# GpSimd takes columns of VectorE's second squaring, and a score burst may wait for VectorE's pair: one core of a gated attention and gMLP kernel

## The chip, the cores and the metric

The kernel runs on one core of a Trainium2 chip. The metric is the device time of one execution in microseconds (us). A core has five engines with a queue of instructions each: TensorE (PE in the profile; its weight loads are PEld), VectorE (DVE), ScalarE (ACT), GpSimd (POOL) and SyncE (SP). Each works through its own queue in order, and engines wait for each other by semaphores. A wait at the head of a queue holds up all that stands behind it.

## The reference

Two branches over the same input are mixed by a gate. The first is attention with 32 query heads of 16 columns over one shared key and value; the second is a gMLP with a mixing matrix over the sequence.

```python
S, D, H, Dh, F, Fh = 2048, 512, 32, 16, 1376, 688      # batch 1
g = sigmoid((x * gate_w).sum(-1, keepdims=True))

q = (x @ wq) as [32 heads, S, 16];  k = x @ wk;  v = x @ wv      # k, v: [S, 16]
p = softmax(q @ k.T * 16 ** -0.5)                                # [32, S, S]
a = (p @ v as [S, 512]) @ wo

z  = gelu(x @ w_in)
z2 = layernorm(z[..., Fh:])
b  = (z[..., :Fh] * (w_sp @ z2 + b_sp[:, None])) @ w_out

out = g * a + (1 - g) * b
```

## The kernel before

**Units and blocks.** Attention's scores are 32 x 2048 x 2048 numbers, and each of them needs an exponential. The work is cut into 32 units. A unit has 64 blocks: 16 tiles of 128 keys times 4 row groups g of TensorE, with 512 columns each. A score pair is two such blocks, two matmuls into two neighbouring banks of PSUM (`s_mm`, tag S).

**Two ways to an exponential.** ScalarE's way (`exp_op`, L579): one instruction reads a pair of banks (128 x 1024, fp32) and writes two slots of the tile P in bf16. It uses banks 0 to 3, two pairs in turn, so the pair for exponential k can be written once exponential k - 2 is done. VectorE's way goes through banks 4 and 5 (BD) and the tile X, which has NX = 5 buffers of 2048 columns in fp16. A batch is four blocks, which are two pairs. For each pair, `d_A` (L603, tag dA) writes a linear function of the scores into half a buffer; then two squarings of the whole buffer (L611, made by `d_poly`) follow. The first (dU) stays in fp16, the second (dW) writes bf16 in place. The square of a square of a linear function, with a small correction by two matmuls for each group (MC, CC), stands for the exponential. A unit gives at most NMAX = 7 of its 16 key tiles to VectorE.

**Values.** TensorE multiplies each block of P or X with V (`pv_mm`, `pv_raw`, tag PV) into bank 6, four row groups side by side, in waves. When a unit is complete, `norm` follows: VectorE transposes the bank into T1 (L623), GpSimd computes the reciprocal (rc, L629), multiplies it with the gate factor (rcg, L632) and scales (Tn, L635). For each second unit VectorE transposes Tn into OT (L638).

**The rest.** The second branch and the projections run as groups of matmuls through bank 7, with an evacuation on VectorE. The GELUs run in one stretch on ScalarE, between about 178 and 205 us, so that its table is loaded only once.

**What sets the order.** A planner in the kernel's own Python fixes the order of every queue before anything runs. It keeps a clock for TensorE, ScalarE and VectorE with assumed costs in ns, asks `pe_pick`, `act_pick` and `dve_pick` in turn for candidates, and takes the ready one with the lowest priority number. GpSimd's instructions go into its queue when the VectorE step that they belong to is chosen. Semaphore waits are derived from reads and writes of keys (`Prog.op`). An operation that needs an earlier one of its own engine waits on that engine's semaphore too, except on TensorE.

Details that matter here:

- `pe_pick` issues a score burst for ScalarE as soon as the banks are free. If VectorE's banks are free too (`d_ok`), VectorE's pair joins the burst behind ScalarE's two matmuls. A pair for VectorE alone is issued when there is time. `dl` is the latest time for the next burst: the planned end of the running exponential less SLATE = 451 ns. Other work for TensorE is only taken when it ends by then.
- `dve_pick` takes, in order of priority, evacuations, norms, dA, other small steps, and last the squarings. The queue of squarings, `polyq`, is strictly first in, first out, and a squaring is assumed to cost 78 + 0.5208 ns for each column.
- When dW ends, the batch's four blocks go to the list `avail` and may be taken into a wave of V matmuls. A batch m cannot begin before batch m - NX has given up its buffer.

Of the kernel before, what the change touches and what calls it, by code (L numbers as in the profile page):

```python
# [15 lines left out]
S = 2048  # L16
# [6 lines left out]
NU = 32  # L23
# [21 lines left out]
PJOIN = 1  # L45
APRI = 1.5
DMARG = 150.0
EMARG = 50.0
EXPT = (0, 478, 904, 1330)
SLATE = 451.0  # L50
# [112 lines left out]
def build_kernel(nc, x_d, wq_d, wk_d, wv_d, wo_d, win_d, wsp_d, bsp_d, wout_d, gw_d, out_d):  # L163
    es = ExitStack()
    with es:
# [423 lines left out]
        def pv_mm(blk, src, key):  # L589
            u, kt, g = blk  # L590
            pv_raw(u, g, V1[:, kt, :], src, [("V", kt // 4), key], "PV")

        def cor_mm(u, g, z):
            n = (64 - units[u]["hi"]) // 4
# [6 lines left out]

        def d_A(m, h):
            op("dve", lambda v: v.tensor_scalar(X[:, m % NX, 1024 * h:1024 * h + 1024], bank(BD, 1024), PA, PB, ALU.mult, ALU.add),  # L603
               r=[bkey(BD), bkey(BD + 1)], w=[("X", m % NX, h)], tag="dA")

        def d_poly(m, hs):

            w = 1024 * len(hs)
            x = X[:, m % NX, 1024 * hs[0]:1024 * hs[0] + w]
            ks = [("X", m % NX, h) for h in hs]  # L610
            return [(78 + 0.5208 * w, lambda d_=d_, tag=tag: op("dve", lambda v: v.tensor_tensor(d_, x, x, ALU.mult), r=ks, w=ks, tag=tag))  # L611
                    for d_, tag in ((x, "dU"), (x.bitcast(B16), "dW"))]

        def norm(pgx, u):
            o = pgx.op
            c, jp, jj = u // 8, (u % 8) // 2, u % 2
            pr = (u // 2) % 2
            t1 = T1[:, :].rearrange("p (b w) -> p b w", w=32)
            lsum = t1[:, :, 16:17]
            tn = Tn[:, pr, :].rearrange("p (b w) -> p b w", w=32)[:, :, 16 * jj:16 * jj + 16]  # L620

            def f_t1():
                o("dve", lambda v: v.transpose(T1[:], bank(BO)), r=[("bk", BO)], w=["T1"], tag="T1")  # L623

            def f_rc(e):
                if e == "dve":
                    o("dve", lambda v: v.reciprocal(rc[:].unsqueeze(2), lsum), r=["T1"], w=["rc"], tag="rc")
                else:
                    o("pool", lambda g: g.tensor_tensor(rc[:].unsqueeze(2), lsum, mone[:].unsqueeze(2), ALU.pow), r=["T1", "mone"], w=["rc"], tag="rc")  # L629

            def f_rcg(e):
                o(e, lambda v: v.tensor_tensor(rcg[:], rc[:], RHO[:, c, :], ALU.mult), r=["rc", ("RHO", c)], w=["rcg"], tag="rcg")  # L632

            def f_tn(e, s_, k):
                o(e, lambda v: v.tensor_tensor(tn, t1[:, :, 0:16], s_[:].unsqueeze(2).broadcast_to([128, 16, 16]), ALU.mult), r=["T1", k], w=[("Tn", pr, jj)], tag="Tn")  # L635

            def f_t2():
                o("dve", lambda v: v.transpose(OT[:, c, jp, :], Tn[:, pr, :]), r=[("Tn", pr, 0), ("Tn", pr, 1)], w=[("OT", c, jp)], tag="T2")  # L638

            if pgx is not pg:  # L640
                return [f_t1, lambda: f_rc("dve"), lambda: f_tn("dve", rc, "rc")] + ([f_t2] if jj else [])
            res = []
            if u < NU - 1:
                def f_all():
                    f_t1()
                    f_rc("pool")
                    f_rcg("pool")
# [69 lines left out]
        dpair = {"free": 0.0}  # L717
        da_q = deque()
        batches = []
        cur = {"m": None, "hs": []}  # L720
# [17 lines left out]
        def new_batch(now):  # L738
# [20 lines left out]
                return True  # L759
            return False  # L760

        def d_pair(now, used):

            if not cur["hs"] and not new_batch(now):
                return None
            m = cur["m"]
            u, kt = batches[m]
            fr = [h for h in cur["hs"] if 2 * h not in used]
            if not fr:
                return None  # L770
            h = fr[0]

            def take():
                cur["hs"].remove(h)
                for i in range(2):
                    s_mm(BD + i, (u, kt, 2 * h + i))
                dpair["free"] = None
                return (m, h)
            return take

        def d_ok(now):
            return dpair["free"] is not None and dpair["free"] + LAT + DMARG <= now and sum(x[0] for x in polyq) <= DPQ

        class Done(dict):
            def get(self, k):
# [11 lines left out]
        def pe_pick(now):  # L797
# [23 lines left out]
            elif ua < NU and edone.get(k - 2) is not None:  # L821
# [19 lines left out]
                if bl:  # L841
                    new = []

                    def emit():
                        T["now"] = now
                        tk = d_pair(now, [b[2] for b in bl]) if d_ok(now) else None
                        for i_, blk in enumerate(bl):
                            s_mm(EB[k % 2] + i_, blk)
                            units[blk[0]]["lo"] += 1
                        if tk:  # L850
                            new.append(tk())
                        stepb[k] = bl
# [197 lines left out]
        def act_pick(now):  # L1050
# [24 lines left out]
            if k in sdone:  # L1075
# [4 lines left out]
                if None not in fr:  # L1080
# [9 lines left out]
                    def f2(t_end):  # L1090
                        edone[k] = t_end
                        for i_, blk in enumerate(bl):
                            avail.append((blk, P[:, 512 * (pp + i_):512 * (pp + i_) + 512], ("P", pp + i_), t_end + LAT + PMARG, k, pp + i_))
                    cands.append((t, 1, EXPT[len(bl)], e2, f2))
            return cands

        def dve_pick(now):
            cands = []
            for q, pr in ((evac_q, 0), (norm_q, 1), (dve_q, 2)):
                if q:  # L1100
# [5 lines left out]

                    def e(q=q, f_=f_):
                        q.popleft()
                        f_()

                    def f(t_end, d_=d_):
# [3 lines left out]
            if da_q:  # L1115
                t, m, h = da_q[0]

                def e1():
                    da_q.popleft()
                    d_A(m, h)  # L1120

                def f1(t_end):
                    dpair["free"] = t_end
                    hs_ = [h]
                    if PJOIN:
                        if m not in half:
                            half[m] = h
                            return
                        hs_ = [0, 1]
                    u, kt = batches[m]  # L1130
                    for z, (c_, f_) in enumerate(d_poly(m, hs_)):
                        polyq.append((c_, f_, m, [(u, kt, 2 * h_ + i) for h_ in hs_ for i in range(2)] if z else []))
                cands.append((t, APRI, 1134, e1, f1))
            if polyq:
                cp_, fp_, mp, rel = polyq[0]

                def e2():
                    polyq.popleft()
                    fp_()

                def f2(t_end):
                    for blk in rel:
                        g = blk[2]
                        avail.append((blk, X[:, mp % NX, 512 * g:512 * g + 512].bitcast(B16), ("X", mp % NX, g // 2), t_end + LAT + PMARG, None, mp))
                cands.append((now, 4, cp_, e2, f2))
            return cands

        half = {}
# [3 lines left out]
        tend = {}  # L1152
        events = [T[k] for k in T if T[k] > 0]
        heapq.heapify(events)
        while True:
# [216 lines left out]
```

## Time and profile before

| | us |
|---|---|
| median of 14 runs | 758.3 |
| lowest and highest run | 755.06 and 767.85 |
| profiled execution | 758.58 |
| its span in the profile | 756.4 |

| engine | busy, us | share of the span |
|---|---|---|
| ScalarE | 734.7 | 97% |
| VectorE | 717.1 | 95% |
| TensorE | 688.2 | 91% |
| GpSimd | 137.3 | 18% |

The lines of the profile are read so. A group of instructions has its source line, engine, operation, the tiles that it writes and reads (output<-input), the shapes, and a count. Behind the first bar are the busy time in us and the mean length of one record in ns; behind the second, the time that the engine was idle just ahead of the group and what ended it. Records of neighbours on ScalarE and VectorE can overlap by some hundred ns: the distance from one start to the next is then shorter than a record. In a timeline, a line has the start in us, the length in us, the engine, and the instruction with its count. In a view by stretches, a line has the stretch, its length, the busy time with the number of instructions, TensorE's granted clock, and the share and rate of DMA.

Where the span ends: the last exponential starts at 745.83 us, and the last unit's norm, the last output projections and the stores take the rest. The GELU stretch holds ScalarE's exponentials from 178.81 to 205.22 us.

### The profile page before, as it was taken

How to read it: one execution, taken by the hardware profiler on the slowest of the kernel's cores; microseconds unless marked ns; L12 is line 12 of the kernel's file. 1: busy time of each engine (PE TensorE's matmuls, PEld its weight loads, DVE VectorE, ACT ScalarE, POOL GpSimd, SP SyncE). 2: the span in 40 equal slices, each digit the busy share in tenths (PEclk: the TensorE clock that was granted, in tenths of full speed). 3: DMA queues.
4: the chain of work that ended last, by engine and by line, in shares of the span. 5: the costliest groups of instructions: out<-in, count | busy, mean ns of one | idle time of the engine just before them, and what ended most of it. 6: DMA issues, size and time to landing. Idle time of an engine off the chain costs nothing.

```text
span 756.4 us, 13353 instructions
## 1 busy us (share of the span) xinstructions
PE 688.2 (91%) x5313; PEld 186.4 (25%) x5407; DVE 717.1 (95%) x784; ACT 734.7 (97%) x801; POOL 137.3 (18%) x112
## 2 busy tenths in 40 slices
PE   7889898889889999999999999899999999999996
PEld 2222222223322222222222222222222222222221
DVE  4599999999999999999999999999999999999996
ACT  5999999999899999999999999999999999999995
POOL 3111101212111111210221111012212112012120
PEclk9899999999999999999999999999999999999999
DMA  9810000000000000310000014000000600000000
GB/s 221 165 23 1 1 1 1 1 1 1 1 1 1 1 1 1 84 42 16 2 1 1 1 31 96 15 1 1 1 1 2 115 19 8 1 1 1 1 1 32
DMA packets 49045, 16.96 MB, mean 22 GB/s; under 512 B 44129, under 2 KB 48913, under 8 KB 48978
## 3 DMA queue, kind: packets, MB, share of 16 engines
q1 hardware_dynamic: 46066, 15.10, 9.2%
q10 hardware_dynamic: 2784, 0.69, 0.5%
q8 instruction: 44, 0.72, 0.4%
q0 software_dynamic: 128, 0.26, 0.2%
q14 instruction: 23, 0.19, 0.1%
HBM read 3.20 MB, written 2.10 MB: 7 GB/s over the span
## 4 chain that ended last, share of the span: by engine, by line
ACT 62%; issue 17%; PE 12%; DVE 7%; DMA 1%; POOL 1%; ACTq 0%
ACT P L579 59%; PE ps L298 8%; PE ps L297 4%; DVE X L603 3%; DVE X L611 2%; ACT z L492 1%; DMA wvg<-in_gate_w_dram 1%; ACT z L496 1%; POOL rc L629 0%; DVE T L623 0%; DVE outsb L556 0%; DVE MC L450 0%; DVE OT L638 0%; ACTq L151 0%; ACT L579 0%
## 5 line engine op out<-in xcount | busy, mean ns | idle before, releaser
L579 ACT ACTIVATE P<-ps 128x1024 bf16<-128x1024 f32 x770 | 707.6, 1152 | 4.0 <-PE ps L298 3.9
L298 PE MATMUL ps<-QA,KA 32*128 32x512 bf16 x2048 | 318.7, 385 | 49.1 <-ACT P L579 40.5
L603 DVE TENSOR_SCALAR X<-ps 128x1024 f16<-128x1024 f32 x254 | 308.8, 1216 | 7.8 <-PE ps L298 6.5
L611 DVE TENSOR_TENSOR X<-X 128x2048 f16<-128x2048 f16 x254 | 311.2, 1226 | 2.6
L629 POOL TENSOR_TENSOR rc<-T,mone 128x16 f32<-128x16 f32 x31 | 97.2, 3134 | 551.6 <-DVE T L623 551.6
L298 PEld LDWEIGHTS ps<-QA,KA 32*128 32x128 bf16 x2048 | 77.2, 91 | 333.6 <-ACT P L579 311.0
L298 PE MATMUL ps<-P,V 128*32 128x512 bf16 x1540 | 138.4, 386 | 0.5 <-DVE T L623 0.5
L297 PE MATMUL ps<-wT,z 128*128 128x512 bf16 x344 | 110.7, 385 | 4.0 <-issue 4.0
L298 PE MATMUL ps<-X,V 128*32 128x512 bf16 x508 | 62.9, 386 | 0.3 <-DVE T L623 0.3
L297 PEld LDWEIGHTS ps<-wT,z 128*128 128x128 bf16 x384 | 26.6, 97 | 59.0 <-issue 55.2
L298 PEld LDWEIGHTS ps<-P,V 128*32 128x32 bf16 x1540 | 28.4, 94 | 41.3 <-issue 39.8
L297 PE MATMUL ps<-win,xT 128*128 128x344 bf16 x128 | 29.8, 314 | 0.2 <-issue 0.2
L297 PE MATMUL ps<-wout,z 128*128 128x512 bf16 x84 | 26.6, 384 | 0.9 <-issue 0.8
L623 DVE STREAM_TRANSPOSE T<-ps 128x512 f32<-128x512 f32 x32 | 22.7, 710 | 2.4 <-PE ps L298 2.4
L297 PE MATMUL ps<-xT,win 128*128 128x512 bf16 x93 | 21.9, 380 | 0.9 <-ACT z L492 0.5
L297 PE MATMUL ps<-wo,OT 128*128 128x512 bf16 x56 | 18.6, 384 | 2.3 <-DVE OT L638 1.3
L635 POOL TENSOR_TENSOR Tn<-T,rcg 128x256 bf16<-128x256 f32 x31 | 20.2, 651 | 2.4
L298 PEld LDWEIGHTS ps<-X,V 128*32 128x32 bf16 x508 | 14.9, 94 | 20.9 <-issue 18.1
L297 PE MATMUL ps<-xT,wq 128*128 128x512 bf16 x55 | 18.3, 386 | 0.9 <-DVE z L527 0.4
L486 DVE CAST z<-ps 128x344 bf16<-128x344 f32 x32 | 16.4, 512 | 0.5 <-PE ps L297 0.2
L527 DVE TENSOR_TENSOR z<-ps,z 128x512 bf16<-128x512 f32 (+1 forms) x24 | 16.3, 678 | 0.4 <-PE ps L297 0.4
L501 DVE BATCH_NORM_STATS2 bst<-z 128x6 f32<-128x344 bf16 x32 | 15.8, 495 | 0.5
(102 smaller groups left out, 248.8 us busy)
## 6 DMA issues: line engine op xcount, KB each, us to landing
out_dram<-outsb SPq DMA_DIRECT2D x15, 128.0 KB, 1.7
win<-in_B_w_in_dram SPq DMA_DIRECT2D x2, 688.0 KB, 6.4
wout<-in_B_w_out_dram SPq DMA_DIRECT2D x1, 640.0 KB, 8.8
wo<-in_A_wo_dram SPq DMA_DIRECT2D x1, 512.0 KB, 7.5
wq<-in_A_wq_dram ACTq DMA_DIRECT2D x1, 384.0 KB, 7.3
wT<-in_B_w_sp_dram SPq DMA_TRANSPOSE x16, 4.6
KA<-KA POOLq DMA_DIRECT2D x4, 64.0 KB, 3.1
wq<-in_A_wq_dram ACTq DMA_DIRECT2D x1, 128.0 KB, 3.9
```

The costliest lines, as they stand in the source:

```text
L297: return t.matmul(dst, lhsT, rhs, start=start, stop=stop)
L298: return t.matmul(dst, lhsT, rhs, start=start, stop=stop, tile_position=tp)
L486: ev = lambda: op("dve", lambda v: v.tensor_copy(z2[:, FH * st + 344 * h:FH * st + 344 * h + 344], bank(BM, 344)), r=[BMK], w=[("z2", st)] ...
L492: op("act", lambda a: a.activation(z1[:, ft, 1024 * (i % 2):1024 * (i % 2) + 1024], bank(b, 1024), ACT.Gelu_apprx_tanh), r=[bkey(b), bkey( ...
L501: dve_q.append((530, lambda st=st, h=h: op("dve", lambda v: v.bn_stats(bst[:, st, h, :], z2[:, FH * st + 344 * h:FH * st + 344 * h + 344]) ...
L527: ev = lambda: op("dve", lambda v: v.tensor_tensor(dst, ps[0:n, 512 * BM:512 * BM + 512], dst, ALU.mult), r=[BMK, ("z1", ft)], w=[("u", ft ...
L579: op("act", lambda a: a.activation(P[:, 512 * p:512 * (p + n)], ps[:, 512 * b0:512 * (b0 + n)], ACT.Exp), r=[bkey(b0 + i) for i in range(n ...
L603: op("dve", lambda v: v.tensor_scalar(X[:, m % NX, 1024 * h:1024 * h + 1024], bank(BD, 1024), PA, PB, ALU.mult, ALU.add), r=[bkey(BD), bke ...
L611: return [(78 + 0.5208 * w, lambda d_=d_, tag=tag: op("dve", lambda v: v.tensor_tensor(d_, x, x, ALU.mult), r=ks, w=ks, tag=tag)) for d_, ...
L623: o("dve", lambda v: v.transpose(T1[:], bank(BO)), r=[("bk", BO)], w=["T1"], tag="T1")
L629: o("pool", lambda g: g.tensor_tensor(rc[:].unsqueeze(2), lsum, mone[:].unsqueeze(2), ALU.pow), r=["T1", "mone"], w=["rc"], tag="rc")
L635: o(e, lambda v: v.tensor_tensor(tn, t1[:, :, 0:16], s_[:].unsqueeze(2).broadcast_to([128, 16, 16]), ALU.mult), r=["T1", k], w=[("Tn", pr, ...
```

## The change

**GpSimd's pieces.** The last 2 x GE = 768 columns of a batch's buffer get keys of their own, in pieces of GE = 384. After dU of a batch, its two last pieces are put into a queue `gq`. Whenever `dve_pick` issues a dA and GpSimd is free by the planner's account (`pool_free`), one piece is taken from the queue, and GpSimd squares it from fp16 to bf16 (`g_piece`, tag gW). The piece is issued just ahead of the dA and is made to wait for the VectorE operation that precedes this dA. The planner books GLAT + 130 + 2.05 x 384 ns for it, and 4700 ns for the norm's three operations. When dW is issued, it leaves out the pieces that are already taken, and at most one more if `gmore` holds; pieces not counted on are dropped from the queue. The batch's blocks go to `avail` when dW and all its pieces are done (`release`).

**Order of the squarings.** A squaring that follows an operation of its own batch directly is now taken as ready only DRAW = 115 ns later, and a squaring of another batch in `polyq` is preferred to it. `d_ok` counts what is left in `polyq` with 1145 ns for each squaring.

**The burst's wait.** If VectorE's banks come free after ScalarE's banks but no later than `dl` (RIDE = 0), and there is a batch to be continued or begun, the time of ScalarE's burst is set to when VectorE's banks are free, so that both pairs go in one burst.

```diff
+DRAW = 115.0
+RIDE = 0.0
+GE = 384
+GLAT = 160.0
+GNS = (130.0, 2.05)
...
-        def d_poly(m, hs):
-
-            w = 1024 * len(hs)
-            x = X[:, m % NX, 1024 * hs[0]:1024 * hs[0] + w]
...
+        XC = [0, 1024, 2048 - 2 * GE, 2048 - GE, 2048] if GE else [0, 1024, 2048]
...
+        def d_square(m, eng, hi, tag):
+
+            x = X[:, m % NX, 0:hi]
+            ks = xkeys(m, 0, hi)
+            op(eng, lambda v: v.tensor_tensor(x if tag == "dU" else x.bitcast(B16), x, x, ALU.mult), r=ks, w=ks, tag=tag)
+
+        def g_piece(m, j):
+
+            lo = XC[2 + j]
+            x = X[:, m % NX, lo:lo + GE]
+            ks = xkeys(m, lo, lo + GE)
+            op("pool", lambda g: g.tensor_tensor(x.bitcast(B16), x, x, ALU.mult), r=ks, w=ks, after=[pg.ops["dve"][-1]], tag="gW")
...
+                    pool_free[0] = max(pool_free[0], T["now"] + 716 + LAT) + 4700
...
-                    cands.append((t, 0, sw("S") + 226, emit, fin, "S"))
                     nxt = edone[k - 1] if edone.get(k - 1) is not None else edone[k - 2] + (EXPT[len(stepb[k - 1])] if k - 1 in stepb else 0)
                     dl = max(t, nxt - SLATE)
+                    ride = dpair["end"] + LAT + DMARG
+                    if max(now, t) < ride <= dl - RIDE and (cur["hs"] or new_ok(now)):
+                        t = ride
+                    cands.append((t, 0, sw("S") + 226, emit, fin, "S"))
...
                 def e1():
                     da_q.popleft()
+                    last_d[0] = m
+                    if gq and pool_free[0] <= now:
+                        mg, j = gq.popleft()
+                        g_piece(mg, j)
+                        pool_free[0] = now + GLAT + GNS[0] + GNS[1] * GE
+                        gdue[mg].append(pool_free[0])
+                        release(mg)
                     d_A(m, h)
+                    dpair["end"] = now + 1134
...
+                it = polyq[0]
+                for x_ in polyq:
+                    if x_[0] != last_d[0]:
+                        it = x_
+                        break
...
+                    hi = 512 * DB - GE * (nis + more)
...
+                cands.append((max(now, tend.get("dve", 0.0) + DRAW) if last_d[0] == mp else now, 4, 78 + 0.5208 * hi, e2, f2))
...
+        def gmore(now):
+
+            return (da_q or cur["hs"] or dpair["free"] is None) and pool_free[0] <= now + 800 and st_["ua"] < NU - 1
+
+        def release(m):
+            if m not in wdone or len(gdue[m]) < wdone[m][1]:
+                return
+            t = max([wdone[m][0]] + [x_ + 200 for x_ in gdue[m]])
+            u, kt = batches[m]
+            for g in range(DB):
+                avail.append(((u, kt, g), X[:, m % NX, 512 * g:512 * g + 512].bitcast(B16), xkeys(m, 512 * g, 512 * g + 512), t + LAT + PMARG, None, m))
```

Because the planner lays out everything anew, the order of all engines' queues changes. Counted in both programs up to the end of the main part: 764 exponentials instead of 770, 130 batches for VectorE instead of 127, and 164 pieces on GpSimd. Of the 130 second squarings, 56 have 1664 columns, 54 have 1280, and 20 have all 2048.

More of the change, by code (lines that the diff above doesn't have):

```diff
@@ L587, in pv_raw, with pv_mm @@
             mm(ps[32 * g:32 * g + 32, 512 * BO:512 * BO + 512], lhsT, src, n == 0, n == pvt.get((u, g), 0) - 1, r, [("bk", BO)], tp=(0, 32 * g), tag=tag)
-        def pv_mm(blk, src, key):
+        def pv_mm(blk, src, keys):
             u, kt, g = blk
-            pv_raw(u, g, V1[:, kt, :], src, [("V", kt // 4), key], "PV")
+            pv_raw(u, g, V1[:, kt, :], src, [("V", kt // 4)] + keys, "PV")
         def cor_mm(u, g, z):
@@ L603, in d_A, with xkeys @@
             op("dve", lambda v: v.tensor_scalar(X[:, m % NX, 1024 * h:1024 * h + 1024], bank(BD, 1024), PA, PB, ALU.mult, ALU.add),
-               r=[bkey(BD), bkey(BD + 1)], w=[("X", m % NX, h)], tag="dA")
-        def d_poly(m, hs):
-            w = 1024 * len(hs)
-            x = X[:, m % NX, 1024 * hs[0]:1024 * hs[0] + w]
-            ks = [("X", m % NX, h) for h in hs]
-            return [(78 + 0.5208 * w, lambda d_=d_, tag=tag: op("dve", lambda v: v.tensor_tensor(d_, x, x, ALU.mult), r=ks, w=ks, tag=tag))
-                    for d_, tag in ((x, "dU"), (x.bitcast(B16), "dW"))]
+               r=[bkey(BD), bkey(BD + 1)], w=xkeys(m, 1024 * h, 1024 * h + 1024), tag="dA")
+        XC = [0, 1024, 2048 - 2 * GE, 2048 - GE, 2048] if GE else [0, 1024, 2048]
+        def xkeys(m, lo, hi):
+            return [("X", m % NX, a) for a, b in zip(XC[:-1], XC[1:]) if a < hi and b > lo]
+        def d_square(m, eng, hi, tag):
[7 more added lines that the diff above has]
+            op("pool", lambda g: g.tensor_tensor(x.bitcast(B16), x, x, ALU.mult), r=ks, w=ks, after=[pg.ops["dve"][-1]], tag="gW")
         def norm(pgx, u):
@@ L716, in build_kernel @@
         pfree = [0.0] * NPB
-        dpair = {"free": 0.0}
+        dpair = {"free": 0.0, "end": 0.0}
         da_q = deque()
@@ L760, in new_batch, with new_ok @@
             return False
+        def new_ok(now):
+            m = len(batches)
+            return not (m >= NX and pd_left.get(m - NX, 0) > 0)
         def d_pair(now, used):
@@ L781, in d_ok @@
         def d_ok(now):
-            return dpair["free"] is not None and dpair["free"] + LAT + DMARG <= now and sum(x[0] for x in polyq) <= DPQ
+            return dpair["free"] is not None and dpair["free"] + LAT + DMARG <= now and sum(1145 if x[1] == "dW" else 2290 for x in polyq) <= DPQ
         class Done(dict):
@@ L1092, in f2 @@
                         for i_, blk in enumerate(bl):
-                            avail.append((blk, P[:, 512 * (pp + i_):512 * (pp + i_) + 512], ("P", pp + i_), t_end + LAT + PMARG, k, pp + i_))
+                            avail.append((blk, P[:, 512 * (pp + i_):512 * (pp + i_) + 512], [("P", pp + i_)], t_end + LAT + PMARG, k, pp + i_))
                     cands.append((t, 1, EXPT[len(bl)], e2, f2))
@@ L1108, in e @@
                         q.popleft()
+                        last_d[0] = None
                         f_()
@@ L1119, in e1 @@
                     da_q.popleft()
+                    last_d[0] = m
[5 more added lines that the diff above has]
+                        release(mg)
                     d_A(m, h)
+                    dpair["end"] = now + 1134
                 def f1(t_end):
                     dpair["free"] = t_end
-                    hs_ = [h]
@@ L1125, in f1 @@
[L1125 to L1132, printed above, removed]
+                    if m not in half:
+                        half[m] = h
+                        return
@@ L1133, in dve_pick @@
+                    polyq.append([m, "dU"])
                 cands.append((t, APRI, 1134, e1, f1))
             if polyq:
-                cp_, fp_, mp, rel = polyq[0]
-                def e2():
-                    polyq.popleft()
-                    fp_()
+                it = polyq[0]
[3 more added lines that the diff above has]
+                        break
+                mp, kind = it
+                hi = 512 * DB
+                if kind == "dW" and GE:
+                    nis = len(gdue[mp])
+                    if nis == 0:
+                        gq_m = [x_ for x_ in gq if x_[0] == mp]
+                    more = 0
+                    if gmore(now):
+                        more = len([1 for x_ in gq if x_[0] == mp])
+                        more = min(more, 1)
+                    hi = 512 * DB - GE * (nis + more)
+                    keep_j = more
@@ new lines, in e2 @@
+                def e2():
+                    last_d[0] = mp
+                    d_square(mp, "dve", hi, kind)
+                    if kind == "dU":
+                        it[1] = "dW"
+                        gdue[mp] = []
+                        if GE:
+                            gq.extend([(mp, 1), (mp, 0)])
+                    else:
+                        polyq.remove(it)
+                        left = [x_ for x_ in gq if x_[0] == mp]
+                        for x_ in left:
+                            if GE * (len(gdue[mp]) + 1) + hi > 512 * DB or x_ in left[keep_j:]:
+                                gq.remove(x_)
@@ L1141, in f2 @@
                 def f2(t_end):
[L1142 to L1145, printed above, removed]
-            return cands
-        half = {}
+                    if kind == "dW":
+                        wdone[mp] = (t_end, (512 * DB - hi) // GE if GE else 0)
+                        release(mp)
@@ new lines, in dve_pick @@
+                cands.append((max(now, tend.get("dve", 0.0) + DRAW) if last_d[0] == mp else now, 4, 78 + 0.5208 * hi, e2, f2))
+            return cands
+        gq, gdue, wdone, pool_free = deque(), {}, {}, [0.0]
+        def gmore(now):
+            return (da_q or cur["hs"] or dpair["free"] is None) and pool_free[0] <= now + 800 and st_["ua"] < NU - 1
+        def release(m):
+            if m not in wdone or len(gdue[m]) < wdone[m][1]:
+                return
+            t = max([wdone[m][0]] + [x_ + 200 for x_ in gdue[m]])
+            u, kt = batches[m]
+            for g in range(DB):
+                avail.append(((u, kt, g), X[:, m % NX, 512 * g:512 * g + 512].bitcast(B16), xkeys(m, 512 * g, 512 * g + 512), t + LAT + PMARG, None, m))
@@ L1149, in build_kernel @@
+        half, tend = {}, {}
+        last_d = [None]
         pick = {"pe": pe_pick, "act": act_pick, "dve": dve_pick}
@@ L1151, in build_kernel @@
         idle_rounds = 0
-        tend = {}
         events = [T[k] for k in T if T[k] > 0]
```

## The prediction

> **What bounds the kernel now.** I read the busy shares first, then the costliest groups, then the stretches of the exponential's line, and last the timeline of VectorE and GpSimd where they overlap. Two engines are nearly full:
>
> ```profile
> PE 688.2 (91%) x5313; PEld 186.4 (25%) x5407; DVE 717.1 (95%) x784; ACT 734.7 (97%) x801; POOL 137.3 (18%) x112
> ...
> L579 ACT ACTIVATE P<-ps 128x1024 bf16<-128x1024 f32 x770 | 707.6, 1152 | 4.0 <-PE ps L298 3.9
> ...
> L603 DVE TENSOR_SCALAR X<-ps 128x1024 f16<-128x1024 f32 x254 | 308.8, 1216 | 7.8 <-PE ps L298 6.5
> L611 DVE TENSOR_TENSOR X<-X 128x2048 f16<-128x2048 f16 x254 | 311.2, 1226 | 2.6
> ...
> L635 POOL TENSOR_TENSOR Tn<-T,rcg 128x256 bf16<-128x256 f32 x31 | 20.2, 651 | 2.4
> ```
>
> ScalarE's 770 exponentials have 707.6 us of the 756.4. Their mean record (1152 ns) is longer than their share of the time (919 ns), because neighbours overlap: the distance from one start to the next is what counts. The stretches of L579 alone give it:
>
> ```profile
> 205.00:320.00 115.00, 114.99 (x127) 1.00 0.07 15
> 320.00:440.00 120.00, 119.57 (x131) 1.00 0.04 10
> 440.00:560.00 120.00, 120.00 (x132) 1.00 0.10 23
> 560.00:680.00 120.00, 120.00 (x132) 1.00 0.11 23
> ```
>
> ScalarE is never free here, and 120.00/132 is 0.909 us for one. The commonest distance between two starts in the trace is 0.904, the shortest too. Summed over all exponentials after 60 us (the GELU stretch left out), the excess over 0.904 is 9.7 us, of which 51 distances with 0.06 us or more too much make 7.0. In most of these 51 the exponential starts 0.42 to 0.43 us after its score pair's matmuls start: the pair came late. So the end is set by **the number of exponentials, plus late score pairs**. VectorE is no spare engine either: from 205 to 745 us it is busy 528.8 of 540. The granted clock of TensorE is 1.00 there, so nothing is to be had from it.
>
> **Exponentials.** Counting instructions in both programs: exponentials 770 to 764, first passes over PSUM (dA) 254 to 260, squarings 254 to 260 (130 batches for 127). The six fewer stand on the bound engine: 6 x 0.909 = 5.5 us off, and nothing hides this. TensorE gets nothing: 12 P matmuls become 12 X matmuls, seven keep-warm matmuls change their bank, the number of score matmuls is the same. SyncE's queue is unchanged.
>
> **VectorE.** Second squarings (dW) shrink: 56 to 1664 columns, 54 to 1280, 20 stay at 2048; this is 164 pieces of 384 columns. The price of a column comes from two rows of one kind, L611 (2048 columns, 1226 ns) and the squaring of Q (512 columns, 412 ns): 814/1536 = 0.53 ns. A piece takes 0.204 us off, 164 take 33.4. The three new batches add six dA and six squarings at their cadence of 1.134 (start to start, as in 338.03 to 339.16 below): 13.6. Where a squaring stands directly behind an operation of its own batch, the distance in the trace is 1.255 instead of 1.134; such places go from 76 to 69, 0.8 us off. Sum: 33.4 - 13.6 + 0.8 = 20.6 us less on VectorE. It is not on the path, so I count none of it by itself. What it can bring is fewer late score pairs: the trace charges TensorE at most 6.8 us of idle to waits for X (3.7, 2.6 and 0.5). Bounds of this relief: 0 and 7.0 (all 51 gone). I take 2, near the low end, since most of the 51 follow a full run of TensorE's own work and VectorE's buffers are due in time for most.
>
> **GpSimd's pieces.** Each is issued in front of a dA and waits for the VectorE operation ahead of that dA. Lengths from two rows: rcg (16 columns, 222 ns) and Tn (256 columns, 620 ns when undisturbed) give 1.66 ns a column and so 0.83 us for 384. These have fp32 inputs and the piece 16-bit ones; for the other bound I take the price of a tensor_tensor in the Trainium skill, GPSIMD Engine Reference, section 3 (4497 ns for 2048 columns[...]): 0.97 us, an estimate. I take 0.83 to 0.97. Start: all 31 rc operations begin 0.08 us after the record of the transpose they wait for; a VectorE record outlasts the next start by 1218 - 1134 = 0.084. So a piece runs from about 0.16 to 1.00-1.13 us of a dA.
>
> **A rule against the change.** First the rows, VectorE and GpSimd in three places:
>
> ```profile
> 338.03 1.22 DVE L603 TENSOR_SCALAR X<-ps 128x1024 f16<-128x1024 f32 x1
> 339.16 1.64 DVE L611 TENSOR_TENSOR X<-X 128x2048 bf16<-128x2048 f16 x1
> ...
> 339.10 0.62 POOL L635 TENSOR_TENSOR Tn<-T,rcg 128x256 bf16<-128x256 f32 x1
> ...
> 136.08 1.22 DVE L611 TENSOR_TENSOR X<-X 128x2048 f16<-128x2048 f16 x1
> ...
> 136.23 1.55 POOL L635 TENSOR_TENSOR Tn<-T,rcg 128x256 bf16<-128x256 f32 x1
> ...
> 624.90 1.22 DVE L603 TENSOR_SCALAR X<-ps 128x1024 f16<-128x1024 f32 x1
> ...
> 625.16 0.62 POOL L635 TENSOR_TENSOR Tn<-T,rcg 128x256 bf16<-128x256 f32 x1
> ```
>
> Where Tn starts first, the squaring behind it grows from 1.22 to 1.64; where the squaring was first, Tn grows from 0.62 to 1.55; beside a dA (the last two rows) both keep their length, and no dA of 254 is longer than 1.227. The growth of a squaring is in every such place the rest of Tn less 0.14 us. The Trainium skill, Perfetto Trace Analysis, section "Optimizing Scalar/DVE Operations", says that the two engines share a read port, so that moving work from one to the other might not help. Taken plainly, it costs what the first rows show: a piece met by a squaring at its start would cost up to 0.83 - 0.14 = 0.69 us where it saves 0.204, and 164 of them 113 us. By the last rows a piece under a dA costs nothing until it reaches 1.134 + 0.14 = 1.27 us into it, so until it is 1.11 us long. I go by the row: all 164 stand in front of a dA, and the price of overlap is 0. If that cover fails, 119 of them have an operation with two SBUF inputs directly behind their dA.
>
> **Pieces as waits.** A batch's V matmuls now wait for GpSimd too. 74 pieces are issued at or behind their batch's dW, 49 of them with the very next operation, so such a batch is free about one dA later. Queued behind a waiting X matmul on TensorE is all that follows, the next score pair too. On GpSimd the pieces share the queue with rc, rcg and Tn: 31 follow a Tn directly. That chain takes 2.90 + 0.22 + 0.62 and gaps, but eight of the 31 rc took 3.79, blocked. Cost: 0 if all are on time, and 8 x 0.5 = 4 us if each such chain makes its piece, and through it a score pair, half a dA late. I take 0.5. Tn is waited for by the transposes OT, which are due over 1 us behind it; a piece ahead of rc uses 0.8 of this.
>
> **The wait for the pair.** VectorE's pair shares a burst with ScalarE's in 249 of 254 cases before and 256 of 260 after; the burst's first matmuls are ScalarE's both times, and kind switches on TensorE go from 1494 to 1486. At 0.105 us each (322 ns from start to start against 216 without a switch) this is 0.8 us on an engine off the path. A held burst goes out 451 ns ahead of the planned end of the exponential before, and the trace needs 426. Bounds: -0.8, and 256 x 0.04 = +10 if each ride comes 0.04 us too late. I take +0.5: bursts are placed against the same limit before the change.
>
> **Sum.** 5.5 + 2.0 - 0.5 - 0.5 = 6.5 us off the profiled execution's 758.6 (span 756.4 and 2.2 around it). Its time is 0.3 above the median of 758.3, so the forecast is 758.3 - 6.5 = 751.8, say **752**, with the span near 750. Its own range: 758.3 - 5.5 - 7.0 = 745.8, up to 756.
>
> **Rivals.** *Given back* (0.18): new lateness of pieces and bursts eats what the six exponentials bring, 756 to 760.5, middle 758. For it: TensorE is 93% busy from 320 to 680 us and its order leaves little room. Against it: VectorE gets 20.6 us of room. *Held bursts come late* (0.13): ScalarE waits a little at most of the 256 rides. The sum turns above 5.5/256 = 0.021 us for each; at 0.04 it is 758.3 - 5.5 + 10 = 763. For it: 25 ns of planned room. Against it: ScalarE's pair is the first of its burst and waits for nothing of VectorE's. *Pieces too long* (0.09): at 1.5 us (twice Tn's price a column) each of 119 blocks its successor by 0.39 us, 46 us in all; less 20.6, VectorE has 26 more than now and some 13 to spare, and becomes the bound: 758.3 + 13 = 771. It decides from about 1.4 us a piece. *It doesn't do what it says*: the ride changes few bursts, as counted; this is inside the forecast.
>
> **Chances.** What measurement can tell from no change is 0.3%, 2.3 us. Faster 0.60 (the forecast), within 0.18, slower 0.22 (the two others). From 745 to 763 lie the forecast, the second case and half of the third, about 0.84.
>
> **What would show it.** Right: 764 exponentials at 0.904 to 0.907 us each in the full stretches; the group of pieces at 0.83 to 0.97 us; L603's and L611's successors not above 1.23 us beside pieces; VectorE busy near 697. Wrong: a mean of pieces above 1.1 or squarings of 1.4 and more in numbers; TensorE's idle charged to GpSimd's pieces by more than 2 us; more than 51 late exponentials, or a distance in the stretches above 0.912.

## The result and the profile after

The changed kernel takes 750.57 us (median of 10 runs, 749.03 to 762.67); the kernel before has 757.72 (47 runs). The ratio, taken from the fast runs alone (each within 1.5% of the fastest run of its kernel), is 0.9897 with a 95% interval of 0.987 to 0.9924, so about 7.8 us less. In a second comparison on another occasion it was 0.992 (0.9892 to 0.9947). The forecast was 752 us, with a range of its own from 745.8 to 756.

The profiled execution took 749.0 us with a span of 747.2. The page of the changed kernel, busy times and costliest groups:

```profile
PE 677.8 (91%) x5317; PEld 183.9 (25%) x5407; DVE 700.2 (94%) x796; ACT 728.2 (97%) x795; POOL 271.8 (36%) x276
...
L584 ACT ACTIVATE P<-ps 128x1024 bf16<-128x1024 f32 x764 | 701.2, 1157 | 0.9 <-PE ps L303 0.9
...
L608 DVE TENSOR_SCALAR X<-ps 128x1024 f16<-128x1024 f32 x260 | 316.4, 1217 | 18.1 <-PE ps L303 16.5
L620 DVE TENSOR_TENSOR X<-X 128x2048 f16<-128x2048 f16 (+3 forms) x260 | 285.4, 1103 | 2.4
L627 POOL TENSOR_TENSOR X<-X 128x384 bf16<-128x384 f16 x164 | 135.4, 826 | 357.2 <-DVE X L620 254.5
```

ScalarE has six instructions less and is as full as before. VectorE is 16.9 us less busy although it does more batches, and now waits more for TensorE's pairs ahead of L608 (16.5 us for 6.5): it has room. The second squarings fall apart by width in the groups that keep shapes apart:

```profile
L620 DVE TENSOR_TENSOR X<-X 128x1664 bf16<-128x1664 f16 x56 | 57.9, 1034 | 0.1
L620 DVE TENSOR_TENSOR X<-X 128x1280 bf16<-128x1280 f16 x54 | 44.1, 816 | 0.0
```

The bound is the same as before, as the stretches of L584 alone show (stretch, length, busy and number, clock, DMA):

```profile
320.00:440.00 120.00, 120.00 (x132) 1.00 0.05 13
440.00:560.00 120.00, 120.00 (x132) 1.00 0.10 23
560.00:680.00 120.00, 120.00 (x132) 1.00 0.10 23
```

Again 0.909 us for one exponential: not faster, but fewer.

**One thing has to be taken out first.** TensorE's granted clock is halved for a stretch in many executions of both kernels, and the time follows it: the changed kernel's spans are 747.2 to 748.3 us in the eight runs with a mean clock of 0.997 or more and 749.4 to 751.2 in those at 0.991 to 0.994. The profile that the prediction was made from, of the kernel before, has such a stretch near its start. First the kernel before, then the changed one, in the view by stretches (busy time of PE, PEld, DVE, ACT and POOL with counts, then the clock):

```profile
27.00:34.00 7.00, 6.53 (x48) 1.60 (x41) 4.07 (x7) 5.19 (x8) 0.00 (x0) 0.54 0.68 143
```

```profile
27.00:34.00 7.00, 6.32 (x69) 2.16 (x70) 6.48 (x13) 7.00 (x10) 1.65 (x2) 1.00 0.67 140
```

At 0.54 of the clock ScalarE gets 5.19 us of work in 7. So 756.4 - 747.2 = 9.2 us is more than the change brings. Below, spans are compared among runs with a mean clock of 0.997 or more, called full clock here: the median is 754.3 us before (26 of the 56 runs whose clock is on record) and 747.5 after (8 of 18), **6.8 us less**. The share of such runs is much the same for both kernels, so the medians of all runs can be compared too. The time around the span is 2.1 us before and 1.8 after in these runs; why it falls isn't shown.

### The profile page after: what moved, and what is told of

The parts are those of the page before. It is cut to its first block, busy times and chain, and to the rows that moved or that the text cites. A ratio compares the mean times of both kernels' runs of the same rounds, so it can differ in the third digit from the quotient of the medians.

```text
span 747.2 us, 13743 instructions
## 1 busy us (share of the span) xinstructions
PE 677.8 (91%) x5317; PEld 183.9 (25%) x5407; DVE 700.2 (94%) x796; ACT 728.2 (97%) x795; POOL 271.8 (36%) x276
## 4 chain that ended last, share of the span: by engine, by line
ACT 68%; issue 19%; PE 9%; DVE 2%; DMA 1%; ACTq 0%
ACT P L584 65%; PE ps L303 6%; PE ps L302 3%; ACT z L497 1%; DMA wvg<-in_gate_w_dram 1%; ACT z L501 1%; DVE X L608 0%; DVE X L620 0%; ACTq L156 0%; DVE outsb L561 0%; DVE OT L653 0%; ACT L501 0%; ACT RHO L475 0%; DVE outsb L1270 0%; DVE T L638 0%
## 5 line engine op out<-in xcount | busy, mean ns | idle before, releaser
L584 ACT ACTIVATE P<-ps 128x1024 bf16<-128x1024 f32 x764 | 701.2, 1157 | 0.9 <-PE ps L303 0.9
L303 PE MATMUL ps<-QA,KA 32*128 32x512 bf16 x2048 | 310.1, 384 | 50.6 <-ACT P L584 44.5
L608 DVE TENSOR_SCALAR X<-ps 128x1024 f16<-128x1024 f32 x260 | 316.4, 1217 | 18.1 <-PE ps L303 16.5
L620 DVE TENSOR_TENSOR X<-X 128x2048 f16<-128x2048 f16 (+3 forms) x260 | 285.4, 1103 | 2.4
L627 POOL TENSOR_TENSOR X<-X 128x384 bf16<-128x384 f16 x164 | 135.4, 826 | 357.2 <-DVE X L620 254.5
L303 PEld LDWEIGHTS ps<-QA,KA 32*128 32x128 bf16 x2048 | 74.9, 91 | 331.1 <-ACT P L584 316.8
L302 PE MATMUL ps<-wT,z 128*128 128x512 bf16 x344 | 107.9, 384 | 4.5 <-issue 4.3
```

Of the source, the lines that this page charges most:

```text
L302: return t.matmul(dst, lhsT, rhs, start=start, stop=stop)
L303: return t.matmul(dst, lhsT, rhs, start=start, stop=stop, tile_position=tp)
L584: op("act", lambda a: a.activation(P[:, 512 * p:512 * (p + n)], ps[:, 512 * b0:512 * (b0 + n)], ACT.Exp), r=[bkey(b0 + i) for i in range(n ...
L620: op(eng, lambda v: v.tensor_tensor(x if tag == "dU" else x.bitcast(B16), x, x, ALU.mult), r=ks, w=ks, tag=tag)
L627: op("pool", lambda g: g.tensor_tensor(x.bitcast(B16), x, x, ALU.mult), r=ks, w=ks, after=[pg.ops["dve"][-1]], tag="gW")
```

## The experiments

Nine further kernels were run, the changed kernel once more and the kernel before twice more. Theory A is that of the prediction: the time follows the number of exponentials on ScalarE, and pieces under a dA cost nothing. The rivals are named with each run. In each diff, the changed kernel is the old side, unless it says otherwise. "Excess" is the sum of what the distances between the starts of exponentials have above 0.904 us, behind 60 us and without the GELU stretch where nothing else is said; a distance at least 0.06 us too long is a late pair. "Behind the last" is the time from the start of the last exponential to the end of the span.

### Without pieces

```diff
-GE = 384
+GE = 0
```

> GE = 0: no pieces on GpSimd; the order rule of the squarings and the burst's wait stay. The planner now gives 125 batches and 774 exponentials. Theory A (the time follows the number of exponentials on ScalarE, at 0.904 to 0.909 us each, and pieces under a dA are free): 10 more exponentials than the changed kernel, so 750.6 + 9.1 = 759.7 us, slower than before by about 2. Rival B (VectorE's order and the burst's wait bring the gain by making score pairs less late, the pieces little): 751 to 753.

Measured: 761.16 us (ratio to before 1.0045, 1.0015 to 1.0075). Six runs at full clock have a span of 756.3 to 757.4, median 757.0: 9.5 us more than the changed kernel, where ten exponentials are 9.0. Rival B falls. The time around the span was 3.3 to 3.8 us in this kernel's runs and 1.8 in the changed kernel's; no profile shows what that is. Without pieces, the rest of the change makes the kernel slower: the burst's wait takes two batches from VectorE here (125, where the order rule alone has 127, below).

### Without the burst's wait

```diff
-RIDE = 0.0
+RIDE = 1e9
```

> RIDE set so large that a burst never waits for VectorE's pair; pieces and the order rule stay. 129 batches, 766 exponentials, 158 pieces. Theory A: two more exponentials than the changed kernel, 750.6 + 1.8 = 752.4 us. Rival C (held bursts come late and cost about 0.02 us or more each): 748 or less, since that cost is gone. Rival D (riding saves TensorE more than its count says): 755 or more.

Measured: 758.26 us, ratio 1.0019 (0.9991 to 1.0047). That looks like rival D, but only one of 12 runs had full clock, with a span of 752.4. This is 4.9 us above the changed kernel: 1.8 for two exponentials, and 2.7 behind the last (13.3 us for 10.5). Five more runs, at 0.992 to 0.994, have spans of 754.7 to 756.4, where the changed kernel has 749.4 to 750.2 at such clocks: the medians of these differ by some 6 us, of which 1 to 2 us are in neither term. So rival D isn't excluded for this rest. Why this kernel met halved stretches so often isn't settled. Rival C falls: no cost of held bursts is given back.

### Room that no plan uses

```diff
-..., 4, 78 + 0.5208 * hi, e2, f2))
+..., 4, 78 + 0.5208 * 512 * DB, e2, f2))
```

> The pieces run on GpSimd and the second squarings are as narrow, but the planner books each second squaring at its full width, so that it doesn't know of the room: 126 batches, 772 exponentials, 154 pieces. VectorE gets about 31 us of room on the chip that no plan uses. Theory A: 8 exponentials more than the changed kernel, 750.6 + 7.2 = 757.8 us, less up to 2 for fewer late score pairs. Rival B (room on VectorE is itself the gain): 751 to 753.

Measured: 762.77 us, ratio 1.0086 (1.0055 to 1.0118); at full clock a span of 759.2 (one run). VectorE really is relieved and waits for TensorE (from the page of this kernel):

```profile
L608 DVE TENSOR_SCALAR X<-ps 128x1024 f16<-128x1024 f32 x252 | 306.7, 1217 | 38.9 <-PE ps L303 37.0
```

Its 38.9 us of idle buy little: 43 distances are 0.06 to 0.25 us too long, with 5.5 us, where the kernel before has 49 with 6.2. (Longer ones, 3.1 us, come with a halved stretch near 218 us.) Rival B falls: room by itself is no gain. It is 5 us worse than theory A had it, and 3.9 of these stand behind the last exponential: 14.4 us for 10.5.

### Pieces behind the dA instead of in front

```diff
+                    d_A(m, h)
                     if gq and pool_free[0] <= now:
...
-                    d_A(m, h)
```

> The same plan, 764 exponentials and 164 pieces, but each piece is issued behind its dA and waits for that dA, so it meets the next VectorE operation, which has two SBUF inputs in 119 cases. Theory A (the lock decides, and the placing under a dA makes the pieces free): the squaring is 0.03 us ahead of the piece, so the pieces wait, mean record 1.3 to 1.6 us instead of 0.83, their batches are some 2 us late, TensorE waits for them: 765 to 800 us. Rival (the two engines don't block each other enough to matter): 750.6, within 1.5 us.

Measured: 782.34 us, ratio 1.0314 (1.0262 to 1.0366). The group, from this kernel's page, and a place in its timeline, VectorE first:

```profile
L627 POOL TENSOR_TENSOR X<-X 128x384 bf16<-128x384 f16 x164 | 223.6, 1364 | 337.6 <-DVE X L608 337.4
```

```profile
341.29 1.23 DVE L620 TENSOR_TENSOR X<-X 128x2048 f16<-128x2048 f16 x1
...
341.33 1.86 POOL L627 TENSOR_TENSOR X<-X 128x384 bf16<-128x384 f16 x1 [0.53 <-DVE X L608]
```

The piece begins 0.04 us behind the squaring and takes 1.86 us instead of 0.83, as the squaring keeps it out; beside a squaring of 1280 columns it takes 1.34. VectorE is held up in turn: its 260 squarings take 299.3 us where the changed kernel's took 285.4. What this does to the rest is in the waits of this kernel (who waited for whom, us in total, times, longest):

```profile
PEld ps L303 <- POOL X L627: 23.9, 29, 1.5
...
ACT P L584 <- PE ps L303: 23.0, 37, 1.3
...
PE ps L303 <- POOL X L627: 13.4, 20, 1.0
```

The late pieces hold TensorE's X matmuls, and behind these stand the score pairs: the excess behind 60 us goes from 8.8 to 37.1 us. Of this, 7.1 us lie in two stretches of halved clock (218 to 228 and 628 to 638 us) and 30.0 outside them. With the same 764 exponentials and 164 pieces, moving a piece by one instruction costs 21 us at full clock, and some 28 in this profile. (The medians, 782.34 and 750.57, are 32 apart, but no run of this kernel had full clock.)

### The pieces on VectorE

```diff
-            op("pool", lambda g: ..., after=[pg.ops["dve"][-1]], tag="gW")
+            op("dve", lambda g: ..., tag="gW")
```

> The changed kernel's plan word for word (764 exponentials, 164 pieces in the same places), but the pieces run on VectorE, ahead of their dA. VectorE gets 164 more instructions of 78 + 0.52 x 384 = 0.28 us, 45 us in all. Theory A (GpSimd's taking them is what gives VectorE the room for this plan; about 22 us of room stand between 60 and 740 us): VectorE becomes the bound, 750.6 + 23 = 773 us, 765 to 785. Rival B (VectorE has room in plenty, the new order alone brings the gain): 751 to 755.

Measured: 781.44 us, ratio 1.0297 (1.025 to 1.0345). Theory A holds, also in its size: the excess is 39.4 us, of which 7.9 lie in two stretches of halved clock, so 31.5 remain for the changed kernel's 8.8; that is 23 us more, as expected, and with the halved stretches the median came out 8 us above the 773. The chain of work that ended last, by engine, for the changed kernel and then for this one:

```profile
ACT 68%; issue 19%; PE 9%; DVE 2%; DMA 1%; ACTq 0%
```

```profile
DVE 80%; PE 10%; ACT 5%; issue 3%; DMA 1%; SPq 0%; ACTq 0%
```

VectorE has become the bound. The pieces come ahead of dA and delay the very operation that frees the pair's banks, so score pairs come late in earnest. Distances at least 0.25 us too long are 55, with 25.7 us (44 with 17.8 outside the halved stretches), where the changed kernel has none. In the waits of this kernel:

```profile
PEld ps L303 <- DVE X L608: 33.2, 86, 0.9
```

### The order rule alone

```diff
-RIDE = 0.0
-GE = 384
+RIDE = 1e9
+GE = 0
```

> No pieces and no waiting bursts: only the order rule of the squarings (115 ns behind the own batch, another batch preferred) is left of the change. 127 batches and 770 exponentials, as before the change; squarings directly behind their own batch fall from 76 to 53. Theory A (the number of exponentials decides): the kernel before, 757.2 us, within 1.5. Rival B (less lateness through VectorE's order): 754 or less.

Measured: 760.63 us, ratio 1.0026 (0.9993 to 1.0059). At full clock the median span is 756.2 (five runs), 1.9 more than before. The profile has 8.9 us of excess behind 60 us for 9.4 to 9.7 before, but 14.1 us behind the last for 10.3 to 10.8. So the order rule gains under 1 us and lost 3.6 at the end of this plan. The median is above what either theory allowed: neither counted the end.

### Longer pieces

```diff
-GE = 384
+GE = 512
-GNS = (130.0, 2.05)
+GNS = (195.0, 1.64)
```

> Pieces of 512 columns, booked at 195 + 1.64 x 512 ns: 176 pieces, 764 exponentials as in the changed kernel. From the measured 826 ns for 384 columns and 222 for 16, a piece takes 1.04 us and ends 1.20 us into its dA, before the next operation reads (1.27). VectorE gets some 14 us more room. Theory A: 750.6 us within 1.5, because the exponentials are as many, and no squaring is longer than 1.23 beside a piece. Rival (pieces of this length meet the squarings): VectorE's squarings grow, 753 or more.

Measured: 752.89 us, ratio 0.992 (0.9881 to 0.9959); at full clock a span of 748.2 (five runs), 0.7 above the changed kernel. The median, above theory A's margin, has seven runs at lower clocks in it. A piece takes 1.04 us as worked out, and only one in 176 was blocked (1.755 us). More room with equally many exponentials brings nothing, as with the room that no plan uses.

### More to VectorE

```diff
 (to the one above)
-SOLO = 300.0
-DMARG = 150.0
-SLATE = 451.0
+SOLO = 150.0
+DMARG = 100.0
+SLATE = 500.0
```

> Pieces of 512 columns, and three of the planner's margins changed so that it gives more to VectorE (SOLO 150, DMARG 100) and sends score bursts 49 ns earlier (SLATE 500): 133 batches, 758 exponentials, 154 pieces. Theory A: six exponentials fewer than the changed kernel, 750.6 - 5.4 = 745.2 us, up to 4 more if the rest of the work behind the last exponential grows as it did in the kernels without the wait or without booked room. Theory of lateness (late score pairs come from TensorE's order, which leaves no slack): the late pairs' 6.7 us fall below 4, another 2 to 3 us off.

Measured: 752.42 us, ratio 0.9912 (0.9876 to 0.9947); at full clock spans of 747.6 and 747.0. Six exponentials fewer than the changed kernel, and nothing gained. Late pairs have 6.2 us where the changed kernel has 6.7 and, in its second profile, 5.9, so an earlier burst is not their cure. Where the 5.4 us went shows in ScalarE's timeline at the end, first in the changed kernel, then in this one:

```profile
736.68 1.17 ACT L584 ACTIVATE P<-ps 128x1024 bf16<-128x1024 f32 x1
741.79 1.26 ACT L1273 ACTIVATE outsb<-ps,G 128x512 bf16<-128x512 f32 x2 [3.94 <-PE ps L302]
```

```profile
731.03 1.19 ACT L584 ACTIVATE P<-ps 128x1024 bf16<-128x1024 f32 x1
742.28 1.27 ACT L1273 ACTIVATE outsb<-ps,G 128x512 bf16<-128x512 f32 x2 [10.06 <-PE ps L302]
```

The last exponential starts 5.65 us earlier, and the last output is no earlier, because TensorE still has 40 matmuls of the other branch and the output projection to do, where the changed kernel has 13. These are two rows of TensorE's timeline of this kernel:

```profile
735.65 1.47 PE L302 MATMUL ps<-wout,z 128*128 128x512 bf16 x6 [1.04 <-DVE sq L570]
...
737.61 2.48 PE L302 MATMUL ps<-wout,z 128*128 128x512 bf16 x10
```

### Few exponentials and a short end

```diff
-GE = 384
-GNS = (130.0, 2.05)
-DMARG = 150.0
-EMARG = 50.0
-SLATE = 451.0
+GE = 448
+GNS = (195.0, 1.64)
+DMARG = 100.0
+EMARG = 0.0
+SLATE = 500.0
```

The plan was picked by two counts, exponentials and matmuls behind the last score pair.

> Pieces of 448 columns booked at 195 + 1.64 ns a column, and margins EMARG 0, DMARG 100, SLATE 500: 132 batches, 760 exponentials, and 13 matmuls of the other branch behind the last score pair, as in the changed kernel (the kernel with 758 exponentials had 40 there, and 6 us more behind the last exponential). Theory A with the end counted (0.904 us for each exponential, about 0.22 us for each matmul left to the end): 3.6 us less than the changed kernel run beside it, about 747 us where that has 750.6. Rival (fewer exponentials no longer pay because score pairs come later as VectorE and TensorE fill up): the same as the changed kernel within 1 us.

> The changed kernel again, to stand beside the others on one chip: 0.9897 of the kernel before, 750 to 751 us, and 827 ns for the longest piece.

Measured side by side: 750.0 us (ratio to before 0.9908, 0.9884 to 0.9933) against 751.31 for the changed kernel again (0.992). The intervals overlap, so the medians don't settle it. The runs of this kernel happened to have lower clocks; at like clocks its span is 744.4 at 0.997 (the changed kernel 747.3 and 748.3 at 0.998) and 746.6 at 0.993 (749.4). That is 2.8 to 3.9 us less, with 3.6 expected, though it rests on two runs of this kernel; its profile (744.4) still has a halved stretch of 3.4 us near 30 us.

### The kernel before, again

> The kernel before again, for a profile without a stretch of halved TensorE clock near 27 us. Theory A: the span is then 754 to 755 us; the excess over 0.904 us between exponentials of the first 60 us falls from 4.1 to about 1.4 us, as in the changed kernel, and that of the rest stays at 9 to 10 us, so the stretch of slow clock was chance and not a gain of the change. Rival (the change brings the better start): the excess of the first 60 us stays near 4 us at full clock.

> The kernel before once more, since both its profiles have a stretch of halved TensorE clock in the first 60 us (near 27 us and near 13 us). If this one has none: span 753 to 755.5 us, excess over 0.904 us in the first 60 us about 1.4 us by the theory that the slow clock made the difference to the changed kernel's 1.36, about 4 us by the rival that the change brings the better start; excess behind 60 us 9 to 10 us by both.

The first of the two again met a halved stretch, near 13 us (span 757.9), and tells nothing. The second had none: span 753.8, and ScalarE works through the start.

```profile
27.00:34.00 7.00, 6.41 (x64) 2.46 (x56) 5.97 (x10) 7.00 (x11) 0.00 (x0) 1.00 0.53 105
```

Its excess in the first 60 us is 2.26 us, between the two theories: of the 4.11 in the first profile of this kernel, 1.85 are not there without the slow clock. The 0.9 that remain above the changed kernel (1.36, and 1.34 in its second profile) are the new plan's, or differ from run to run; one profile doesn't tell.

## Why the prediction was right

All told, the mechanism was the forecast one: fewer exponentials on an engine that stayed the bound. The span was forecast near 750 because it was counted from a profile with a halved stretch; 6.5 us off the 754.3 at full clock would be 747.8, and 747.5 was measured. The table sets the spans at full clock beside the sum 747.5 + 0.904 x (exponentials - 764) + (time behind the last - 10.5). The time behind the last is from one profile of each kernel.

| kernel | exponentials | matmuls at the end | behind the last, us | sum, us | span at full clock, us |
|---|---|---|---|---|---|
| before | 770 | 13 | 10.5 | 752.9 | 754.3 |
| changed | 764 | 13 | 10.5 | 747.5 | 747.5 |
| without pieces | 774 | 13 | 10.7 | 756.7 | 757.0 |
| without the burst's wait | 766 | 28 | 13.3 | 752.1 | 752.4 (one run) |
| room unused | 772 | 32 | 14.4 | 758.6 | 759.2 (one run) |
| order rule alone | 770 | 32 | 14.1 | 756.5 | 756.2 |
| longer pieces | 764 | 13 | 10.9 | 747.9 | 748.2 |
| more to VectorE | 758 | 40 | 16.5 | 748.1 | 747.3 |
| few, short end | 760 | 13 | 10.6 | 744.0 | 744.4 (one run) |

The two terms account for each of these variants within 0.8 us, and for the kernel before within 1.4; at full clock, runs of the changed kernel differ by up to 1.1 us and those of the kernel before by 3.0. (The two kernels in which score pairs are held up by pieces are not in the table: there the lateness decides.)

- **Exponentials, 5.5 us.** Right, 5.4 by starts at 0.904. It is four fifths of the gain, and the variants move with it.
- **Fewer late score pairs, 2.0, less 0.5 for pieces and 0.5 for rides: 1.0 together.** Right in sum by luck, with the parts mis-sized. From the undisturbed profile before to the profile after, the span falls by 6.6: 5.4 for the exponentials, 0.9 in the start, 0.6 behind 60 us (9.4 to 8.8), and -0.3 at the first exponential and the end. The 0.9 in the start was in no term. Most late pairs stayed: 56 with 6.7 us and, in the second profile of the changed kernel, 47 with 5.9, where the three profiles of the kernel before have 49 to 56 with 6.8 to 7.5. That is about 0.9 us less, not 2. The trace of before had charged waits for X with up to 6.8 us; but a profile with 38.9 us of idle on VectorE still has late pairs. So the charge for waits was no measure of what relief of VectorE brings. The late exponentials of the changed kernel start 0.42 to 0.43 us behind their pair, as they did before the change, and TensorE's row shows no gap ahead of any of these pairs. What would make these pairs punctual stays open: 49 ns of earlier bursts did not.
- **Pieces.** Measured 825 to 827 ns where 0.83 to 0.97 was expected; the slope between the rows of rcg and Tn was right for 16-bit inputs too. (The 4497 ns for 2048 columns that the prediction takes from the Trainium skill, GPSIMD Engine Reference, section 3, come to 0.84 us for 384 in proportion, not to 0.97.) Of 164, 124 start inside their dA, the median of these 0.16 us into it as expected, and the last one ends 1.00 us into it. What the prediction didn't see: 39 others start up to 0.82 us ahead of their dA, as this still waits for its score pair, and run in part where VectorE is idle. One, behind rstd, met a squaring of 1664 columns and lengthened it from 1.03 to 1.66. The shared read port was rightly weighed by the place: the same pieces one instruction later cost 21 us at full clock.
- **VectorE, 20.6 us less.** Measured 16.9 of busy time. A piece saves what was worked out: 2048, 1664 and 1280 columns take 1225, 1034 and 816 ns. But busy time counts whole records, so the new batches add 12 of 1.22 us, 14.6 instead of 13.6 us, and the gaps within a batch (0.8) don't count; the remaining 2 us are in other groups and in the few squarings that waited for Tn or a piece.
- **Pieces as waits, 0.5.** No wait for a piece is in the list of the changed kernel's waits, which goes down to 0.2 us, so 0 would have been right. No Tn was blocked (618 to 622 ns), though nine of the 31 rc took 3.59 to 3.79.
- **The ride, +0.5.** Wrong in sign, and its worth was looked for in TensorE's switches. It is in the plan: with pieces, riding gives VectorE one batch more (130 for 129) and a shorter end; without pieces it takes away batches (125 for 127).
- **The end** was in no term. It happens to be equal before and after (13 matmuls in both), so the sum held; that was luck too. In four variants it grew by 2.7 to 6 us, nearly as much as the change brings.

## What to carry to other kernels

Work moved to an engine that shares a port with its donor paid here only where the donor's own instruction left the port alone: look in the trace for a pair of rows that overlap without growing, place the work there, and count how long it may be. Freed time on an engine near its limit was worth nothing until the plan turned it into fewer instructions on the engine that sets the end; count those first. Then count what is left behind the last of them, because a better balance in the middle can be lost at the end.

## What the runs showed of the hardware

A stretch of halved TensorE clock (3.4, 6.8, 10.2, 13.7, 20.5, 23.9 or 37.5 us long in these profiles, all multiples of 3.4; at 11 to 36 us, near 215 us, or in the middle) comes in many executions of both kernels, beside the one at the very end. It moves the span by 2 to 13 us, which can be more than this change: the changed kernel has 747.2 at a mean clock of 0.998, 751.0 at 0.991, 760.9 at 0.972. What brings a stretch on isn't shown here. A profile should be read for it ahead of any sum.

VectorE's squarings and GpSimd's pieces kept each other out, whichever came first, for about the whole of the overlap: a squaring that begins 0.04 us ahead of a piece makes the piece's 0.83 us into 1.86, and a piece of 0.83 us that begins 0.05 us ahead of a squaring makes its 1.03 into 1.66. Beside a dA, pieces kept their 825 to 827 ns.
